# Loading x already transposed by DMA, in place of transposing it on TensorE

The chip is one Trainium2; the program runs on one of its cores. The metric is the device time of one execution in microseconds (us), the median over executions. The kernel was already tuned.

## The reference

With S = 2048 rows, D = 640 and F = 1536, all bf16 (the zero is a scalar zero):

```
h   = einsum("bsd,df->bsf", x, w1) + b1
r   = where(h > 0, h, 0)
out = einsum("bsf,fd->bsd", r * r, w2) + b2
```

In both kernels the first-layer matmuls on TensorE (the PE), 128*128 by 128x256 or 128x512 in the traces, read x with D on the partitions, that is, transposed; x lies in DRAM with rows of D.

## The kernel before

The PE's program is a list of events: dummy matmuls ("D") that keep it busy while the first loads come, transposes of one 128-row tile of x ("T"), first-layer groups ("S1", five matmuls into one PSUM bank) and second-layer tiles ("S2", 24 matmuls). The first groups work on two tiles (256 columns), so that work can begin after the first 256 rows; all later ones work on four tiles (512 columns).

```python
    events += [("D",)] * N_DUMMY_0            # 6
    events += [("T", 0), ("T", 1)]
    events += [("D",)] * N_DUMMY_1            # 1
    events += [S1(t01, 0), ("B1T",), S1(t01, 1)]
    events += [S1(t01, 2), ("T", 2), ("T", 3), S1(t01, 3)]
    events += [S1(t23, 0), S1(t23, 1), S1(t23, 2), S1(t23, 3)]
    # ... four-tile groups 4 to 11, with ("T", 4) to ("T", 7) between them
    # ... later tiles: 12 groups each, with T and S2 events between them
```

All the large loads are issued on SyncE, in this order; each `ld_x` of two tiles and each `ld_w1` is 320 KB, `b2` is 160 KB, the others are 640 KB:

```python
            ld_x(0); ld_w1(0); ld_w1(1); ld_x(1)
            ld_w1(2); ld_w1(3); ld_w1(4); ld_w1(5)
            ld_x(2); ld_w2(0); ld_w2(1); ld_w2(2); b2; ld_x(3); ld_x(4)   # condensed
```

A tile's transposes go to a PSUM bank, and VectorE (DVE) copies them to `xT_sb`, which the first layer reads:

```python
                            ins = pe.transpose(out=pv[:, dt, :],
                                in_=x_sb[:, st, dt * P:(dt + 1) * P], identity=ident[:])
# ...
                        dve.tensor_copy(out=xT_sb[:, pc["lo"]:pc["hi"], st * P:(st + 1) * P],
                            in_=psT_view(pc["bank"])[:, pc["lo"]:pc["hi"], :])
```

## Time and profile before

| | before |
|---|---|
| median time, four executions | 119.98 us (119.90 to 120.22) |
| span of the profiled execution | 118.2 us |
| PE busy | 112.3 us (95%) |
| first real matmul | 5.71 us |
| two-tile groups over | 11.81 us |
| first second-layer tile begins | 25.71 us |
| last five second-layer tiles begin | 99.41 us |

The last four rows are places in the timeline and in the chain of waits. They cut the span into a start (to 11.81), a stretch while loads still come (to 25.71), a steady part (to 99.41) and an end. Such cuts let one see where two kernels differ. The lines of the start stand in the prediction; these are the ones of the cuts, from the chain in order of time (start, duration, engine, line, count of instructions):

```profile
9.46 2.34 PE ps L311 x20
...
25.71 3.26 PE ps L331 x24
...
99.41 16.31 PE ps L331 x120
```

In all these views PE stands for matmuls on TensorE, PEld for its weight loads, DVE for VectorE, ACT for ScalarE, SPq for SyncE issuing a load, and L311 for line 311 of the kernel (the first layer; L331 is the second). One more line is needed later, from the page's part 2:

```profile
DMA packets 10281, 9.46 MB, mean 80 GB/s; under 512 B 545, under 2 KB 10273, under 8 KB 10273
```

### The profile page before, as it was taken

The page shows a single profiled execution, that of the slowest core. Times are in us where ns is not written, and L with a number is a line of the kernel's source. Part 1 is how long each engine was busy: PE and PEld are TensorE (multiplying, and loading weights), DVE is VectorE, ACT ScalarE, POOL GpSimd, SP SyncE. Part 2 cuts the span into 40 slices and gives each one's busy share as a digit, 9 for nine tenths or more (in the row PEclk, how much of TensorE's full clock was granted, in tenths as well). Part 3 has the DMA queues.
Part 4 walks back from the last instruction along what each step waited for, and adds up shares of the span by engine and source line. Part 5 has one row for each costly group of instructions (what it writes and reads, how often), then busy time and mean ns, then how long its engine had stood idle before and what let it go on. Part 6 is the DMA issues. An engine that isn't in the chain of part 4 may idle for free.

```text
span 118.2 us, 1743 instructions
## 1 busy us (share of the span) xinstructions
PE 112.3 (95%) x722; PEld 68.1 (58%) x732; DVE 41.7 (35%) x100; ACT 36.2 (31%) x57; POOL 1.4 (1%) x7
## 2 busy tenths in 40 slices
PE   7698998999999999999999999999999999999991
PEld 2377444456575656657565665647465655777770
DVE  0244354432425434231434534142423334211241
ACT  5156644460423315051422406042332406000000
POOL 4000000000000000000000000000000000000000
DMA  3999999400101001010101001010100101011111
GB/s 74 307 324 309 362 364 367 169 4 0 55 6 55 0 0 58 0 58 6 55 0 47 9 0 61 0 55 0 55 0 19 42 0 55 0 55 55 55 61 55
DMA packets 10281, 9.46 MB, mean 80 GB/s; under 512 B 545, under 2 KB 10273, under 8 KB 10273
## 3 DMA queue, kind: packets, MB, share of 16 engines
q1 hardware_dynamic: 10240, 9.34, 24.8%
q8 instruction: 6, 0.10, 0.4%
q14 instruction: 3, 0.02, 0.0%
q0 software_dynamic: 32, 0.00, 0.0%
HBM read 6.72 MB, written 2.62 MB: 79 GB/s over the span
## 4 chain that ended last, share of the span: by engine, by line
PE 90%; DMA 3%; DVE 3%; ACT 2%; issue 1%
PE ps L331 44%; PE ps L311 42%; PE ps L294 3%; DMA x_sb<-in_x_dram 3%; DVE xT_sb L399 2%; ACT r_sb L380 2%; DVE h2T_sb L407 1%; DVE o_sb L423 0%; PE ps L284 0%
## 5 line engine op out<-in xcount | busy, mean ns | idle before, releaser
L311 PE MATMUL ps<-xT_sb,w_sb 128*128 128x512 bf16 (+1 forms) x250 | 54.3, 362 | 1.5 <-DVE xT_sb L399 0.9
L331 PE MATMUL ps<-w_sb,h2T_sb 128*128 128x320 bf16 x384 | 54.1, 299 | 0.0
L380 ACT ACTIVATE r_sb<-ps,b1T_sb 128x512 bf16<-128x512 f32 (+1 forms) x52 | 34.0, 655 | 59.4 <-PE ps L311 59.1
L331 PEld LDWEIGHTS ps<-w_sb,h2T_sb 128*128 128x128 bf16 x384 | 37.5, 98 | 16.0
L311 PEld LDWEIGHTS ps<-xT_sb,w_sb 128*128 128x128 bf16 x260 | 24.7, 98 | 23.5 <-DVE xT_sb L399 1.5
L407 DVE TENSOR_TENSOR h2T_sb<-r_sb 128x512 bf16<-128x512 bf16 (+1 forms) x52 | 21.1, 405 | 35.6 <-ACT r_sb L380 35.3
L423 DVE TENSOR_TENSOR o_sb<-ps,b_bc 128x320 bf16<-128x320 f32 x32 | 14.3, 487 | 34.2 <-PE ps L331 34.2
L399 DVE COPY xT_sb<-ps 128x640 bf16<-128x640 bf16 (+1 forms) x16 | 7.5, 476 | 4.7 <-PE ps L294 4.7
L294 PEld LDWEIGHTS ps<-ident,x_sb 128*128 128x128 bf16 x80 | 5.5, 101 | 5.7 <-DVE xT_sb L399 1.9
L294 PE MATMUL ps<-ident,x_sb 128*128 128x128 bf16 x80 | 7.0, 225 | 1.2 <-DMA x_sb<-in_x_dram 0.6
L280 PE MATMUL ps<-const-bfloat16-1.0 128*128 128x512 bf16 x7 | 3.1, 588 | 0.8 <-PEq L444 0.8
L280 PEld LDWEIGHTS ps<-const-bfloat16-1.0 128*128 128x128 bf16 x7 | 0.8, 128 | 1.9 <-issue 1.9
L353 ACT ACT_TABLE_LOAD x1 | 1.3, 1283 | 0.7 <-PEq L444 0.7
L363 ACT ACTIVATE xT_sb<-ps 128x128 bf16<-128x128 bf16 x2 | 0.6, 278 | 2.6 <-PE ps L294 2.6
L261 POOL DMA_DIRECT2D b_sb<-in_b_dram x1 | 0.6, 647 | 0.8 <-POOLq L444 0.8
L375 ACT ACTIVATE b1T_sb<-ps 128x12 f32<-128x12 bf16 x1 | 0.2, 182 | 1.2 <-PE ps L284 1.2
L264 POOL TENSOR_SCALAR_AFFINE_SELECT ident<-ident 128x128 bf16<-128x128 bf16 x1 | 0.3, 289 | 0.2 <-POOL ident L262 0.2
L262 POOL MEMSET ident<- 128x128 bf16 x1 | 0.2, 233 | 0.0
L284 PEld LDWEIGHTS ps<-ident,b_sb 12*128 12x128 bf16 x1 | 0.1, 90 | 0.2 <-issue 0.2
L353 ACT ACTIVATE scr_act<-const-float32-0.0 128x1 f32<-128x1 f32 x1 | 0.2, 203 | 0.0
L284 PE MATMUL ps<-ident,b_sb 12*128 12x12 bf16 x1 | 0.2, 176 | 0.0
L444 POOL MEMSET const-bfloat16-1.0<- 128x1 bf16 x1 | 0.1, 108 | 0.0
(3 smaller groups left out, 0.3 us busy)
## 6 DMA issues: line engine op xcount, KB each, us to landing
out_dram<-o_sb SPq DMA_DIRECT2D x15, 160.0 KB, 1.8
w_sb<-in_w_dram SPq DMA_DIRECT2D x6, 320.0 KB, 6.1
x_sb<-in_x_dram SPq DMA_DIRECT2D x3, 640.0 KB, 10.5
w_sb<-in_w_dram SPq DMA_DIRECT2D x3, 640.0 KB, 8.1
x_sb<-in_x_dram SPq DMA_DIRECT2D x2, 320.0 KB, 4.3
b_bc<-in_b_dram SPq DMA_DIRECT2D x1, 160.0 KB, 8.6
out_dram<-o_sb SPq DMA_DIRECT2D x2, 80.0 KB, 1.6
b_sb<-in_b_dram POOLq DMA_DIRECT2D x1, 3.0 KB, 3.7
```

Of the source, the lines that this page charges most:

```text
L261: pool.dma_start(b1_sb[:], b1v).then_inc(sem_b1, 16)
L280: pe.matmul(ps[:, DBANK, :], lhsT=c_lhs, rhs=c_rhs, start=True, stop=True)
L284: pe.transpose(out=psB, in_=b1_sb[:], identity=ident[0:NFT, 0:NFT]).then_inc(sem_peb1, 1)
L294: ins = pe.transpose(out=pv[:, dt, :], in_=x_sb[:, st, dt * P:(dt + 1) * P], identity=ident[:],)
L311: ins = pe.matmul(ps[:, bank, 0:wdt], lhsT=w1_sb[:, dt, ft * P:(ft + 1) * P], rhs=xT_sb[:, dt, s0:s0 + wdt], start=(dt == 0), stop=(dt == ...
L331: return pe.matmul(ps[:, b0 + h, 0:HALF], lhsT=h2T_sb[:, ft, st * P:(st + 1) * P], rhs=w2_sb[:, ft, h * HALF:(h + 1) * HALF], start=(ft == 0),
L353: act.activation(out=scr_act[:, 0:1], in_=c_f32, func=AF.Relu)
L363: act.activation(out=xT_sb[:, pc["lo"]:pc["hi"], st * P:(st + 1) * P], in_=psT_view(pc["bank"])[:, pc["lo"]:pc["hi"], :], func=AF.Copy,).t ...
L380: act.activation(out=r_sb[:, k % NR, 0:wdt], in_=ps[:, k % NS1B, 0:wdt], func=AF.Relu, bias=b1T_sb[:, ft:ft + 1], scale=1.0,).then_inc(sem ...
L399: dve.tensor_copy(out=xT_sb[:, pc["lo"]:pc["hi"], st * P:(st + 1) * P], in_=psT_view(pc["bank"])[:, pc["lo"]:pc["hi"], :],).then_inc(sem_x ...
L407: dve.tensor_tensor(out=h2T_sb[:, ft, s0:s0 + wdt], in0=r_sb[:, k % NR, 0:wdt], in1=r_sb[:, k % NR, 0:wdt], op=ALU.mult,).then_inc(sem_D1, 1)
L423: ins = dve.tensor_tensor(out=o_sb[:, st, h * HALF:(h + 1) * HALF], in0=ps[:, b0 + h, 0:HALF], in1=b2_bc[:, h * HALF:(h + 1) * HALF], op=A ...
```

## The change

The intent is to take the 80 transposes off the PE and the 18 copies off DVE and ScalarE: SyncE issues transposing loads straight into `xT_sb`. The diff, cut to its core:

```diff
-    NS1B = 3
+    NS1B = 4
-    N_DUMMY_0 = 6
-    N_DUMMY_1 = 1
+    N_DUMMY_0 = 9
     events += [("D",)] * N_DUMMY_0
-    events += [("T", 0), ("T", 1)]
-    events += [("D",)] * N_DUMMY_1
     (all other "T" events, their PE transposes and their copies removed too)
         def need_xT_tiles(W, tiles):
             for st in tiles:
-                for pc in tile_pieces[st]:
-                    need_piece_evacuated(W, pc)
+                W.need(sem_x[x_dma_of_tile(st)], 16)
             def ld_x(i):
                 t0, n = x_dmas[i]
-                src = x2[t0 * P:(t0 + n) * P, :].rearrange("(st p) d -> p st d", p=P)
-                sp.dma_start(x_sb[:, t0:t0 + n, :], src).then_inc(sem_x[i], 16)
+                sp.dma_start_transpose(
+                    out=xT_sb[:, :, t0 * P:(t0 + n) * P], in_=x2[t0 * P:(t0 + n) * P, :]
+                ).then_inc(sem_x[i], 16)
```

The order of the loads is unchanged. The bank that held transposes becomes a fourth bank for the first layer.

More of the change, by code (lines that the diff above doesn't have):

```diff
@@ L34, in bass_standalone__dense_activation_squared_relu__prompt_kernel @@
     NR = 4
-    NS1B = 3
-    TBANK = 3
+    NS1B = 4
     S2BANK0 = 4
@@ L39, in bass_standalone__dense_activation_squared_relu__prompt_kernel @@
     B1BANK = 2
-    N_DUMMY_0 = 6
-    N_DUMMY_1 = 1
-    SPLIT_AT = 4
+    N_DUMMY_0 = 9
     x_dmas = [(0, 2), (2, 2), (4, 4), (8, 4), (12, 4)]
@@ L63, in bass_standalone__dense_activation_squared_relu__prompt_kernel @@
     events += [("D",)] * N_DUMMY_0
-    events += [("T", 0), ("T", 1)]
-    events += [("D",)] * N_DUMMY_1
     t01, t23, t03 = [0, 1], [2, 3], [0, 1, 2, 3]
     events += [S1(t01, 0), ("B1T",), S1(t01, 1)]
-    events += [S1(t01, 2), ("T", 2), ("T", 3), S1(t01, 3)]
+    events += [S1(t01, 2), S1(t01, 3)]
     events += [S1(t23, 0), S1(t23, 1), S1(t23, 2), S1(t23, 3)]
-    events += [S1(t03, 4), S1(t03, 5)]
-    events += [S1(t03, 6), ("T", 4), S1(t03, 7), ("T", 5)]
-    events += [S1(t03, 8), ("T", 6), S1(t03, 9), ("T", 7)]
-    events += [S1(t03, 10), S1(t03, 11)]
+    events += [S1(t03, ft) for ft in range(4, NFT)]
     for c in range(1, 4):
@@ L77, in bass_standalone__dense_activation_squared_relu__prompt_kernel @@
             events.append(S1(tiles, g))
-            if c + 1 < 4 and g in (4, 6, 8, 10):
-                events.append(("T", 4 * (c + 1) + (g - 4) // 2))
             if g in (2, 5, 8, 11):
@@ L84, in bass_standalone__dense_activation_squared_relu__prompt_kernel @@
     LAST_S2 = events[-1][1]
-    t_order = [ev[1] for ev in events if ev[0] == "T"]
     s1_groups = [ev[1:] for ev in events if ev[0] == "S1"]
@@ L90, in bass_standalone__dense_activation_squared_relu__prompt_kernel @@
     s2_index = {st: i for i, st in enumerate(s2_order)}
-    assert sorted(t_order) == list(range(NST)) and sorted(s2_order) == list(range(NST))
+    assert sorted(s2_order) == list(range(NST))
     assert len(s1_groups) == len(set(s1_groups))
@@ L99, in bass_standalone__dense_activation_squared_relu__prompt_kernel @@
     tile_last_group = {st: max(cells[(st, ft)] for ft in range(NFT)) for st in range(NST)}
-    def t_pieces(st):
-        if st == 0:
-            return [(0, SPLIT_AT, TBANK, "dve"), (SPLIT_AT, NDT, TBANK + 1, "act")]
-        if st == 1:
-            return [(0, SPLIT_AT, TBANK + 2, "dve"), (SPLIT_AT, NDT, TBANK + 3, "act")]
-        if st == 2:
-            return [(0, NDT, TBANK, "dve")]
-        if st == 3:
-            return [(0, NDT, TBANK + 1, "dve")]
-        return [(0, NDT, TBANK, "dve")]
-    pieces = []
-    for st in t_order:
-        for (lo, hi, bank, eng) in t_pieces(st):
-            pieces.append(dict(st=st, lo=lo, hi=hi, bank=bank, eng=eng))
-    cnt = {"dve": 0, "act": 0}
-    last_in_bank = {}
-    for pi, pc in enumerate(pieces):
-        pc["pe_idx"] = pi
-        pc["prev"] = last_in_bank.get(pc["bank"])
-        last_in_bank[pc["bank"]] = pc
-        cnt[pc["eng"]] += 1
-        pc["evac_cnt"] = cnt[pc["eng"]]
-    tile_pieces = {st: [pc for pc in pieces if pc["st"] == st] for st in range(NST)}
-    EARLY_T_BANK_PIECES = [pc for pc in pieces if pc["bank"] >= S2BANK0]
     s2_pe_after = {}
@@ L159, in sem @@
             return es.enter_context(nc.semaphore(name))
-        x_sb = sb("x_sb", [P, NST, D], BF16)
         xT_sb = sb("xT_sb", [P, NDT, S], BF16)
@@ L186, in bass_standalone__dense_activation_squared_relu__prompt_kernel @@
         sem_b1T = sem("sem_b1T")
-        sem_T = sem("sem_T")
-        sem_xT = sem("sem_xT")
-        sem_xTa = sem("sem_xTa")
         sem_S1 = sem("sem_S1")
@@ L195, in bass_standalone__dense_activation_squared_relu__prompt_kernel @@
         sem_out = sem("sem_out")
-        def psT_view(bank):
-            return ps[:, bank, :].bitcast(BF16)[:, 0:NDT * P].rearrange("p (a b) -> p a b", a=NDT)
         psB = ps[:, B1BANK, :].bitcast(BF16)[:, 0:NFT]
-        evac_sem = {"dve": sem_xT, "act": sem_xTa}
-        def need_piece_evacuated(W, pc):
-            W.need(evac_sem[pc["eng"]], pc["evac_cnt"])
         def need_xT_tiles(W, tiles):
             for st in tiles:
-                for pc in tile_pieces[st]:
-                    need_piece_evacuated(W, pc)
+                W.need(sem_x[x_dma_of_tile(st)], 16)
         @block.sync
@@ L284, in _ @@
                     pe.transpose(out=psB, in_=b1_sb[:], identity=ident[0:NFT, 0:NFT]).then_inc(sem_peb1, 1)
-                elif kind == "T":
-                    st = ev[1]
-                    W.need(sem_ident, 1)
-                    W.need(sem_x[x_dma_of_tile(st)], 16)
-                    for pc in tile_pieces[st]:
-                        if pc["prev"] is not None:
-                            need_piece_evacuated(W, pc["prev"])
-                        pv = psT_view(pc["bank"])
-                        for dt in range(pc["lo"], pc["hi"]):
-                            ins = pe.transpose(
-                                out=pv[:, dt, :],
-                                in_=x_sb[:, st, dt * P:(dt + 1) * P],
-                                identity=ident[:],
-                            )
-                        ins.then_inc(sem_T, 1)
                 elif kind == "S1":
@@ L324, in _ @@
                         W.need(sem_D2, d2_after[s2_order[i - 2]])
-                    for pc in EARLY_T_BANK_PIECES:
-                        need_piece_evacuated(W, pc)
                     b0 = S2BANK0 + 2 * (i % 2)
@@ L356, in _ @@
                 kind = ev[0]
-                if kind == "T":
-                    st = ev[1]
-                    for pc in tile_pieces[st]:
-                        if pc["eng"] != "act":
-                            continue
-                        W.need(sem_T, pc["pe_idx"] + 1)
-                        act.activation(
-                            out=xT_sb[:, pc["lo"]:pc["hi"], st * P:(st + 1) * P],
-                            in_=psT_view(pc["bank"])[:, pc["lo"]:pc["hi"], :],
-                            func=AF.Copy,
-                        ).then_inc(sem_xTa, 1)
-                elif kind == "S1":
+                if kind == "S1":
                     s0, wdt, ft = ev[1:]
@@ L392, in _ @@
                 kind = ev[0]
-                if kind == "T":
-                    st = ev[1]
-                    for pc in tile_pieces[st]:
-                        if pc["eng"] != "dve":
-                            continue
-                        W.need(sem_T, pc["pe_idx"] + 1)
-                        dve.tensor_copy(
-                            out=xT_sb[:, pc["lo"]:pc["hi"], st * P:(st + 1) * P],
-                            in_=psT_view(pc["bank"])[:, pc["lo"]:pc["hi"], :],
-                        ).then_inc(sem_xT, 1)
-                elif kind == "S1":
+                if kind == "S1":
                     s0, wdt, ft = ev[1:]
```

## The prediction

> **What bounds the kernel now.** I read the page first (busy shares and the chain of waits), then the chain in order of time, then the timeline of the first microseconds, then the busy time of the PE in stretches.
>
> ```profile
> PE 112.3 (95%) x722; PEld 68.1 (58%) x732; DVE 41.7 (35%) x100; ACT 36.2 (31%) x57; POOL 1.4 (1%) x7
> ...
> DMA  3999999400101001010101001010100101011111
> ...
> PE 90%; DMA 3%; DVE 3%; ACT 2%; issue 1%
> PE ps L331 44%; PE ps L311 42%; PE ps L294 3%; DMA x_sb<-in_x_dram 3%; DVE xT_sb L399 2%; ACT r_sb L380 2%; DVE h2T_sb L407 1%; DVE o_sb L423 0%; PE ps L284 0%
> ...
> L294 PE MATMUL ps<-ident,x_sb 128*128 128x128 bf16 x80 | 7.0, 225 | 1.2 <-DMA x_sb<-in_x_dram 0.6
> ```
>
> The PE is the bound: it is on the chain for 90% of the span, and nothing else has more than 3%. The DMA engines are full in slices 2 to 7 (to about 21 us) and nearly idle afterwards. L294 is the 80 transposes that the change takes away. Its 7.0 us of busy time are not its price, since neighbouring matmuls overlap there; 3% of the span, 3.6 us, is nearer to it. The chain in order of time gives the unit prices:
>
> ```profile
> 31.12 0.28 PE ps L294 x5
> ...
> 92.92 3.26 PE ps L331 x24
> 96.17 3.24 PE ps L311 x15
> ```
>
> One tile's five transposes cost 0.28 us of PE time in the steady part, a first-layer group over four tiles (five matmuls) 3.24/3 = 1.08 us, and a second-layer tile (24 matmuls) 3.26 us. The start is different. The timeline has:
>
> ```profile
> 0.75 0.43 SPq L217 DMA_DIRECT2D x_sb<-in_x_dram  x1
> ...
> 1.24 1.02 SPq L221 DMA_DIRECT2D w_sb<-in_w_dram  x2
> ...
> 2.30 0.53 SPq L217 DMA_DIRECT2D x_sb<-in_x_dram  x1
> ...
> 2.87 4.43 SPq L221 DMA_DIRECT2D w_sb<-in_w_dram  x4
> ...
> 4.12 0.98 PE L294 MATMUL ps<-ident,x_sb 128*128 128x128 bf16 x10 [0.61 <-DMA x_sb<-in_x_dram]
> ...
> 5.71 0.70 PE L311 MATMUL ps<-xT_sb,w_sb 128*128 128x256 bf16 x5 [0.40 <-DVE xT_sb L399]
> ...
> 9.46 0.71 PE L311 MATMUL ps<-xT_sb,w_sb 128*128 128x256 bf16 x5 [0.54 <-DVE xT_sb L399]
> ```
>
> The first x load is issued at 0.75 and lands at 3.98; ten transposes and the copies out of PSUM follow, and the first real matmul runs at 5.71. The groups over tiles 2 and 3 begin at 9.46 and end at 11.81. The view of issues with their landings, narrowed to single issues, gives 3.9 us for the first w1 block (lands 1.24 + 3.9 = 5.1), 4.8 for the second (1.7 + 4.8 = 6.5), 5.3 for the second x load (2.30 + 5.3 = 7.6) and 5.9 for the third w1 block (8.8). So behind one another, 320 KB land every 1.1 to 1.4 us, as in a queue.
>
> [...] The trace of before has 0.28/5 = 0.056 us of path for one PE transpose in sequence[...]. [...] Before's plain loads moved 316 GB/s in the stretch 5.71 to 11.86. [...]
>
> **The change part by part.**
>
> Removed, steady part (tiles 4 to 15). Between 11.86 and 25.71 the PE does 11 first-layer groups (eight over tiles 0 to 3, three of the next four tiles) and four tiles' transposes: 13.85 - 11 x 1.08 = 1.97 us for the transposes, their switching and their waits for bank 3 to be emptied. Between 25.71 and 99.41 it does 33 groups, 11 second-layer tiles and eight tiles' transposes: 73.70 - 33 x 1.08 - 11 x 3.26 = 2.2 us, which agrees with 8 x 0.28. All of it lies on the path: **4.2 us** saved, 3.5% of the time. The 16 copies on DVE (7.5 us busy) and two on ACT vanish beside the PE, which costs and saves nothing more. A fourth bank for the first layer loosens a wait that the trace does not show; worth nothing.
>
> Removed at the start: ten transposes and their copies between 3.98 and 5.71 (1.7 us), then the second ten (about 0.8 us of path) and a 0.54 us wait for their copies.
>
> Added at the start: x must land transposed, and everything behind it in the queue waits too. The first-layer groups over two tiles need the first x load and the first w1 block; those over tiles 2 and 3 the second x load. I call the transposing rate R. The plain load's 320 KB took 1.1 us behind others. [...] at 150 GB/s 2.2 us (+1.1), at 100 GB/s 3.3 us (+2.2). With d the excess, the first w1 block lands at 5.1 + d, the second x load at 7.6 + 2d. The four groups over tiles 0 and 1 take some 2.6 us, the four over tiles 2 and 3 then 2.35.
> [...]
> - R = 150: first matmul 6.2, second half from 9.8 (the load lands last) to 12.1: 0.3 us lost; 3.9 gained, 116.1 us.
> - R = 100: first matmul 7.3, second half from 12.0 to 14.3: 2.5 us lost, and the last third of w2 comes some 1.4 us late (x of tiles 4 to 7 takes 6.6 us instead of 2.2 ahead of it): about 119.7 us.
>
> Moved: the dummy matmuls are nine in place of seven. At 0.427 us each from 0.79 they end near 4.7, before any of these first matmuls, so they delay nothing and keep the PE busy up to a gap of 0.6 to 2.6 us. All the later x loads have slack: tiles 8 to 15 land before 25 us in the kernel before and are now needed after 48 us.
>
> **The rivals.**
>
> (a) [...] The steady 4.2 us and the start's 1.4 us both come: 113.9 to 114.8 us. [...] Against it: the pieces are 256 B, not the 1280 B rows of before[...].
>
> (b) The transposing load is the new wait. Below about 100 GB/s the wait for x at the start, and again for the next four tiles near 22 us behind a queue in order, eats the 4.2 us. At 60 GB/s a 320 KB load takes 5.5 us (d = 4.4): first matmul at 9.5, after a gap of nearly 5 us[...]; second x load at 16.4; start lost by 7 us, and x and w2 still late afterwards: 124 to 130 us. For it: all loads stand in one queue, and the first slices already run the DMA engines at 90% and more.
>
> (c) SyncE's issue becomes the bound. [...] one issue takes microseconds, the w1 block behind it is issued late, and the start loses 2 to 5 us even though the DMA engines have room: 118 to 121 us.
>
> (d) Nothing is gained, since the transposes were hidden anyway. Against it: they are on the chain, and the PE has under 1% of idle time between 25.71 and 99.41. I leave it little.
>
> **Range and chances.** The removed 4.2 us is near certain; the whole doubt is the start, that is R. I give [...] rather over a quarter to 150 to 220 (115 to 116), a sixth to 110 to 150 (116 to 118.5), and some three tenths to slower loads or slow issues (119 and up, with a long tail). The middle of this is 116.0 us; eight in ten lie between 114.2 and 124.0. Faster by over 2% is below 117.6: 0.65. Within 2% (117.6 to 122.4): 0.13. Slower: 0.22.
>
> **What would show it.** Right: no L294 and no copies into xT; the chain between second-layer tiles holds only 3.24 and 3.26 us pieces; the PE's first real matmul at 5.3 to 6.5 us, released by the DMA of x or w1; a wait on the DMA of x before the groups over tiles 2 and 3 of at most 1.5 us[...]. Wrong: landing of the first x load well over 5 us after its issue, a DMA wait of the PE of several us at the start or near 22 us, issues of several us on SyncE, first matmuls at half clock. If the chain between 26 and 99 us is not about 2.2 us shorter, the removal step is wrong.

## The result, and the profile after

| | before | after |
|---|---|---|
| median time | 120.18 us (16 executions, 119.72 to 121.80) | 116.75 us (11 executions, 115.37 to 118.05) |
| ratio of fast runs | | 0.967 (0.964 to 0.971) |

The ratio is the mean time of one kernel's fast runs over that of the other's of the same rounds, so not quite the ratio of the medians quoted. The kernel is 3.3% faster and it scatters more: its executions lie near 115.4 to 115.8, 116.6 to 117.3 and 118.1 us. The profiled one (118.1 us, span 116.3) belongs to the slow ones. The kernel before has slow executions too, but fewer here: one of sixteen took 121.8 us. First its page: engines, packets and chain by engine and by line (L247 is the first layer, L265 the second):

```profile
PE 110.8 (95%) x645; PEld 65.5 (56%) x654; DVE 35.4 (30%) x84; ACT 35.7 (31%) x55; POOL 1.4 (1%) x7
...
DMA packets 18551, 9.44 MB, mean 81 GB/s; under 512 B 10864, under 2 KB 18544, under 8 KB 18544
...
PE 92%; DMA 4%; SPq 1%; issue 1%; DVE 0%
PE ps L247 47%; PE ps L265 45%; DMA w_sb<-in_w_dram 4%; SPq L166 1%; DVE o_sb L336 0%; PE ps L235 0%
```

The transposes and copies are gone. The chain has two new links at its start: SyncE's issue of the transposing load (L166) and the landing of a **w1** block, not of x. The packets under 512 B grew by 10,319. That fits 2048 rows times five blocks of 128 columns, 10,240 pieces of 256 B: what was a row of 1280 B is now five pieces.

The timeline of the start, of the same kernel (start, duration, engine, line, what):

```profile
0.75 1.34 SPq L166 DMA_TRANSPOSE xT_sb<-in_x_dram  x1
...
0.79 4.00 PE L231 MATMUL ps<-const-bfloat16-1.0 128*128 128x512 bf16 x9 [0.79 <-PEq L357]
...
2.16 1.13 SPq L172 DMA_DIRECT2D w_sb<-in_w_dram  x2
...
6.49 1.23 PE L247 MATMUL ps<-xT_sb,w_sb 128*128 128x256 bf16 x5 [1.70 <-DMA w_sb<-in_w_dram]
...
7.76 6.39 PE L247 MATMUL ps<-xT_sb,w_sb 128*128 128x256 bf16 x35
```

Three things are to be seen. The issue of the first x load takes 1.34 us (0.43 before), so the first w1 block is issued at 2.16 instead of 1.24 and lands at 6.35 (2.16 and 4.2 to landing), while x landed at 4.45 (0.75 and 3.7). The dummies end at 4.79, and the PE stands idle for 1.70 us. And then the matmuls are slow: five of 256 columns take 1.23 us, against 0.70 in the kernel before, and the two-tile groups are over at 14.15 instead of 11.81.

The steady part, in the chain in order of time:

```profile
26.02 3.26 PE ps L265 x24
29.29 3.24 PE ps L247 x15
...
97.50 16.32 PE ps L265 x120
```

From 26.02 to 97.50 are 71.48 us; before they were 73.70 (25.71 to 99.41). Nothing but matmuls of the two layers is left there.

### The profile page after: what moved, and what is told of

Read it like the earlier page. It is cut to its first block, busy times and chain, and to the rows that moved or that the text cites. A ratio compares the mean times of both kernels' runs of the same rounds, so it can differ in the third digit from the quotient of the medians.

```text
span 116.3 us, 1569 instructions
## 1 busy us (share of the span) xinstructions
PE 110.8 (95%) x645; PEld 65.5 (56%) x654; DVE 35.4 (30%) x84; ACT 35.7 (31%) x55; POOL 1.4 (1%) x7
## 4 chain that ended last, share of the span: by engine, by line
PE 92%; DMA 4%; SPq 1%; issue 1%; DVE 0%
PE ps L247 47%; PE ps L265 45%; DMA w_sb<-in_w_dram 4%; SPq L166 1%; DVE o_sb L336 0%; PE ps L235 0%
## 5 line engine op out<-in xcount | busy, mean ns | idle before, releaser
L247 PE MATMUL ps<-xT_sb,w_sb 128*128 128x512 bf16 (+1 forms) x251 | 55.8, 378 | 2.2 <-DMA w_sb<-in_w_dram 1.7
L265 PE MATMUL ps<-w_sb,h2T_sb 128*128 128x320 bf16 x384 | 54.1, 299 | 0.0
L265 PEld LDWEIGHTS ps<-w_sb,h2T_sb 128*128 128x128 bf16 x384 | 37.6, 98 | 16.5
L247 PEld LDWEIGHTS ps<-xT_sb,w_sb 128*128 128x128 bf16 x260 | 26.7, 103 | 28.3 <-issue 2.6
L231 PE MATMUL ps<-const-bfloat16-1.0 128*128 128x512 bf16 x9 | 4.0, 626 | 0.8 <-PEq L357 0.8
```

The costliest lines, as they stand in the source:

```text
L231: pe.matmul(ps[:, DBANK, :], lhsT=c_lhs, rhs=c_rhs, start=True, stop=True)
L247: ins = pe.matmul(ps[:, bank, 0:wdt], lhsT=w1_sb[:, dt, ft * P:(ft + 1) * P], rhs=xT_sb[:, dt, s0:s0 + wdt], start=(dt == 0), stop=(dt == ...
L265: return pe.matmul(ps[:, b0 + h, 0:HALF], lhsT=h2T_sb[:, ft, st * P:(st + 1) * P], rhs=w2_sb[:, ft, h * HALF:(h + 1) * HALF], start=(ft == 0),
```

## The experiments

The state of the PE clock was the suspect for the scatter (the profiler records which share of the full TensorE clock was granted), and the rival was that loads land at varying times. A program on one core is listed as slow when a run is over 1.5% above the fastest of its kernel.

### The changed kernel again

No edit. The first repeat:

> The changed kernel once more, unaltered, because its profiled execution fell in the slow state (116.3 us span) and its runs scatter from 115.4 to 118.1 us while the kernel before stays near 120.2. Theory 1 (the PE starts cold: dummies end at 4.8, the first real matmul comes at 6.5, and after that gap the PE runs its 256-column matmuls at about 213 ns instead of 108 until a moment that differs from execution to execution): a faster execution must show fewer slow 256-column matmuls, and the span must differ by just that; from 26 us on nothing differs. Theory 2 (the loads of x and w1 land at varying times): the first real matmul or a DMA wait moves by the difference, 1 to 2 us. Time 115.4 to 118.1 us again.

Measured: 115.37, 117.00, 117.07 and 117.11 us; ratio 0.969 (0.961 to 0.977). The profiled one was again called slow, but its record of the granted clock shows the cause. The view cuts the time into stretches; columns are the stretch and its length, busy time of PE, PEld, DVE, ACT and POOL, the granted PE clock, DMA share and GB/s:

```profile
6.84:8.00 1.16, 1.16 (x7) 0.64 (x8) 0.00 (x0) 0.00 (x0) 0.00 (x0) 0.59 1.10 195
8.00:9.00 1.00, 1.00 (x7) 0.69 (x7) 0.23 (x1) 0.65 (x2) 0.00 (x0) 0.50 1.12 278
9.00:10.00 1.00, 1.00 (x6) 0.75 (x5) 0.32 (x2) 0.47 (x1) 0.00 (x0) 0.50 1.15 269
10.00:11.00 1.00, 1.00 (x9) 0.78 (x7) 0.23 (x2) 0.47 (x1) 0.00 (x0) 0.77 1.12 303
11.00:12.00 1.00, 1.00 (x11) 0.90 (x10) 0.39 (x2) 0.92 (x2) 0.00 (x0) 1.00 1.20 305
```

The granted clock is one half from about 7.05 to 10.46 us (0.59 and 0.77 are mixtures of 1 and 0.5), one stretch of 3.4 us. Half of that is 1.7 us, which is 1.5% of the span: the mean clock of 0.985 that this run lists. These 1.7 us are also the distance of this execution (117.11) from the fastest (115.37). The start of the same execution:

```profile
0.79 3.50 PE L231 MATMUL ps<-const-bfloat16-1.0 128*128 128x512 bf16 x9 [0.79 <-PEq L357]
6.84 1.05 PE L247 MATMUL ps<-xT_sb,w_sb 128*128 128x256 bf16 x5 [2.55 <-DMA w_sb<-in_w_dram]
```

Nine dummies took 3.50 us here, against 4.00 in the first profile. So the PE had become fast during the dummies, idled for 2.55 us, and lost the clock just as the real work began.

The second repeat asked for a fast run's profile:

> The changed kernel once more, to get a profile of an execution that was not slow. By the theory of the cold PE a fast execution (115.4 us) has the same landings as the slow ones (first w1 block at 6.3 to 6.7, same gap before the first real matmul) but 256-column matmuls of about 108 ns from the first or second group on, so 4.4 to 5.2 us for forty in place of 6.3 to 7.7, and from the first second-layer tile on the same chain.

Measured: 116.83 and 117.16 us, ratio 0.971 (0.963 to 0.979), both with mean clock 0.985. They are called fast only because they are measured against each other; among the executions of the result 117.17 us was called slow. The execution expected at 115.4 did not come, so no execution of that group was ever profiled. The profiled one (span 115.4) took as long as that of the first repeat (115.3), and serves below for the account of the stages. Its stretch view:

```profile
4.80:6.90 2.10, 0.11 (x1) 0.13 (x2) 0.00 (x0) 0.00 (x0) 0.00 (x0) 1.00 1.30 306
6.90:10.40 3.50, 3.50 (x22) 2.47 (x21) 0.88 (x3) 1.61 (x4) 0.00 (x0) 0.66 1.07 257
```

The drop comes a little later here (about 8.0 us, by the same sum), so the first five matmuls ran at full speed (0.70 us) and later ones not. Its gap was 2.03 us and its first matmul came at 6.79 us; the landing of w1 hence moves by 0.3 us between executions (6.35 to 6.7), much less than the scatter. Its chain has these cuts:

```profile
7.61 5.59 PE ps L247 x35
...
25.07 3.26 PE ps L265 x24
...
96.54 16.31 PE ps L265 x120
```

The account of this execution against the kernel before, from the chains: two-tile groups over at 13.20 against 11.81 (1.39 lost), then 11.87 to the first second-layer tile against 13.90 (2.03 saved), then 71.47 against 73.70 (2.23 saved), and an end of 18.86 against 18.79. The sum is 2.80 us, the difference of the spans (118.2 and 115.4).

### Fourteen dummies

```diff
-    N_DUMMY_0 = 9
+    N_DUMMY_0 = 14
```

> Fourteen dummy matmuls in place of nine, nothing else. They end between 6.0 and 6.8 us, so the gap before the first real matmul (6.5) is closed. Theory 1 (cold PE after the gap): the 40 matmuls of 256 columns take 4.4 to 5 us instead of 7.7, the groups over tiles 2 and 3 end near 11 us instead of 14.15, the time falls to 114.3 to 115.3 us and the scatter shrinks to a few tenths. Theory 2 (the loads set the start): no gain, or up to 0.3 us of loss, and the same scatter.

Measured: 115.42 us median of six, from 115.28 to 115.49, 0.1 us above the range of theory 1; ratio 0.960 (0.957 to 0.964). The group of the forty 256-column matmuls (busy time and mean ns after the bar), of the first profile of the changed kernel and then of this one:

```profile
L247 PE MATMUL ps<-xT_sb,w_sb 128*128 128x256 bf16 x40 | 7.6, 375 | 1.7 <-DMA w_sb<-in_w_dram 1.7
```

```profile
L247 PE MATMUL ps<-xT_sb,w_sb 128*128 128x256 bf16 x40 | 4.7, 273 | 0.1
```

The loads were left as they were: in this run the first w1 block landed at 6.4 (2.13 and 4.3). Only the gap was filled with PE work, and the slow matmuls and the scatter of some 2.7 us both vanished. The theory of varying loads falls. The time is that of the fastest executions of the changed kernel (115.37). That these are the ones whose real matmuls ran at full speed is the likely reading; none was profiled. The mean clock alone does not tell: of the twelve executions of the result, the profiled one included, the four from 116.83 to 117.31 us list 0.985; the three fastest list 1.00, but so do three near 116.7 and the two slowest near 118.1.

### A control without any transposing DMA

The kernel before with two dummies in place of six ahead of the first transposes:

```diff
-    N_DUMMY_0 = 6
+    N_DUMMY_0 = 2
```

> The kernel before with two dummy matmuls in place of six ahead of the first transposes: a control for the cold PE without any DMA transpose. The PE then idles from about 1.7 to 4.1 us. If an early idle gap keeps the PE slow for a varying time, this kernel becomes 0.5 to 3 us slower than the kernel before (120.6 to 123 us), with 256-column matmuls of about 213 ns apart well past 6 us, and it scatters as the changed kernel does. If the slow matmuls of the changed kernel have to do with its DMA traffic, this stays at 120 us.

Measured: 121.50 us (121.19 to 121.59), ratio 1.011 (1.009 to 1.014): the same by the 2% rule, but clear of 1. The timeline of this variant:

```profile
0.79 1.01 PE L280 MATMUL ps<-const-bfloat16-1.0 128*128 128x512 bf16 x2 [0.79 <-PEq L444]
3.85 1.23 PE L294 MATMUL ps<-ident,x_sb 128*128 128x128 bf16 x10 [2.06 <-DMA x_sb<-in_x_dram]
...
6.93 2.31 PE L311 MATMUL ps<-xT_sb,w_sb 128*128 128x256 bf16 x10
```

Ten 256-column matmuls take 2.31 us here, about twice the 1.27 us of the kernel before. Too little PE work early on thus makes the PE slow with plain loads too, and transposing loads are not needed for it. The edit lengthens the gap by taking work away, so it does not tell a long gap from little work; nor does the edit to fourteen dummies, which does both the other way round. The expected scatter did not come: all six executions were slow by the same amount. The recorded clock is 1.00 throughout in this run. So there are two forms of the loss: a PE that became fast only late (not seen in the record of the clock, only in the durations; in the first profile of the changed kernel it was slow to about 12 us, and the record read 1.00 while five 256-column matmuls took 1.23 us instead of 0.70), and one that became fast and fell back (seen as 0.985). The unaltered kernel before also has executions near 121.7 us with a recorded clock of 1.00 (one to four of eleven in the three groups of rounds of these experiments). They took about as long as this control; none was profiled, so their cause is not shown.

### Transposing by DMA in the steady part alone

The kernel before, with tiles 0 to 3 untouched and tiles 4 to 15 loaded by transposing DMA:

```diff
             def ld_x(i):
                 t0, n = x_dmas[i]
+                if t0 >= 4:
+                    sp.dma_start_transpose(out=xT_sb[:, :, t0 * P:(t0 + n) * P],
+                        in_=x2[t0 * P:(t0 + n) * P, :]).then_inc(sem_x[i], 16)
+                    return
     (their "T" events removed; their groups wait for sem_x)
```

> The kernel before with only tiles 4 to 15 loaded transposed by DMA; tiles 0 to 3 keep plain loads, PE transposes and copies, so the start is that of before. It prices the steady part alone: by the prediction 4.2 us less than the kernel before, so 115.7 to 116.1 us, with the scatter of the kernel before, and a chain from 11.86 to 97.3 us of matmuls alone. If the transposes were in fact hidden behind something else in the steady part, less is gained; if the transposing loads of later tiles come too late, a DMA wait appears near 20 to 25 us.

Measured: 115.93 us median, 0.964 (0.959 to 0.968); four executions from 115.56 to 115.93 and two slow ones near 117.6, which were not profiled. Beside the kernel before in the same rounds (120.10), that is 4.2 us less, as expected. The chain of this variant, where L314 and L334 are the two layers:

```profile
9.26 14.21 PE ps L314 x75
23.47 3.26 PE ps L334 x24
...
94.94 16.31 PE ps L334 x120
```

After 9.26 us no DMA wait and no copy is left. From there to the last five second-layer tiles are 85.68 us, against 89.95 in the kernel before (9.46 to 99.41), which is 4.3 us less. So 4.2 to 4.3 us is the gain of the steady part, and in the changed kernel the start gave some of it back.

### Plain loads of the same bytes

The changed kernel with plain loads in the place of the transposing ones; the output is wrong on purpose, since the rows aren't transposed.

```diff
-                sp.dma_start_transpose(
-                    out=xT_sb[:, :, t0 * P:(t0 + n) * P], in_=x2[t0 * P:(t0 + n) * P, :]
-                ).then_inc(sem_x[i], 16)
+                src = x2[t0 * P:(t0 + n) * P, :].rearrange("(p a) d -> p (a d)", p=P)
+                src = src.rearrange("p (dt c) -> p dt c", dt=NDT)
+                sp.dma_start(xT_sb[:, :, t0 * P:(t0 + n) * P], src).then_inc(sem_x[i], 16)
```

> The changed kernel with plain loads of the same bytes in the same order in place of the transposing ones (the output is wrong on purpose: the rows are not transposed). It shows what transposing by DMA costs by itself, with the nine dummies kept. The first load then lands at 4.0 and the first w1 block at 5.1 as in the kernel before, so the gap after the dummies (4.8) is 0.3 us. If the cost of the start is in the transposing loads (slower landing, longer issue on SyncE), the first real matmul comes at 5.1 to 5.3, the PE is warm by about 6, and the time is 113.6 to 114.4 us. If the order of loads and the missing transposes alone made the start slow, it stays at 116 to 117 us. SyncE's issue of an x load should fall from 1.34 to about 0.43 us.

Measured: 115.67 us (115.08 to 116.62), 0.965 (0.958 to 0.972). The issue took 0.63 us and the first real matmul came at 5.75 us, both later than expected, after a gap of 1.18 us. The executions fall into two pairs, 115.1 and 116.2 to 116.6. The result lies between the two expectations. The profiled execution (115.2) ran its first matmuls at full speed and lost 0.51 us to a wait for the second w1 block; the slower pair was not profiled, so what of the result is due to the loads and what to the clock stays open. The first real matmul of the changed kernel came at 6.49 to 6.84 us in its three profiles, so in this order of loads the transposing load makes it 0.7 to 1.1 us late (one profile of the plain loads).

### The first w1 block ahead of x

```diff
-    N_DUMMY_0 = 9
+    N_DUMMY_0 = 11
-            ld_x(0)
-            ld_w1(0)
+            ld_w1(0)
+            ld_x(0)
             ld_w1(1)
```

> The changed kernel with the first w1 block issued ahead of the first x load, and eleven dummy matmuls (they end near 5.3 us). In the changed kernel the transposing load held SyncE for 1.34 us, so the first w1 block was issued at 2.16 and landed at 6.35, and it was this that the first real matmul waited for; x itself had landed at 4.45. If the long issue is what makes the start late, w1 now lands at about 4.2 and x near 5.0, the first real matmul comes at 5.1 to 5.6 and the time falls to 114.0 to 114.6 us (fourteen dummies alone gave 115.4). If the DMA engines' rate is what limits the start, both orders deliver the two blocks at the same time, near 6.3, and the time stays at 115.3 to 115.6 us.

Measured: 114.73 us (114.38 to 114.98), 0.956 (0.953 to 0.958). The timeline of this variant:

```profile
0.75 0.45 SPq L172 DMA_DIRECT2D w_sb<-in_w_dram  x1
1.26 1.46 SPq L166 DMA_TRANSPOSE xT_sb<-in_x_dram  x1
```

w1 lands at 4.15 (0.75 and 3.4) and x at 5.36 (1.26 and 4.1). Both are there one microsecond earlier than in the changed kernel (6.35), with the same bytes through the same engines. So it was the long issue in front of w1, and not the rate of the DMA engines, that made the first matmul late. The time is 0.1 us above the expected range; the first five matmuls took 0.95 us, not yet at full speed.

The same with nine dummies asks how much of a gap is harmful:

> The kernel with the first w1 block ahead of the first x load, with nine dummies in place of eleven: a gap of about 0.5 us before the first real matmul (from 4.8 to 5.4) in place of none. If any gap there keeps the PE slow in some executions, the time becomes 114.7 to 117 us with a scatter of over 1 us; if only gaps of well over 1 us do, it stays at 114.5 to 115 us with little scatter.

Measured: 114.37 us (114.18 to 115.51), 0.951 (0.946 to 0.956). It is the fastest version, though its interval overlaps that of eleven dummies. (In these rounds an execution of the kernel before at 121.72 us counts as fast, which lowers this ratio and the next a little.) The gap was longer than expected: the dummies became fast on their way and ended at 4.3, so the PE waited 1.29 us for x, and in the profiled execution the matmuls were at full speed nevertheless. A gap of 1.3 us is thus not a certain loss. One execution of six took 115.5 us; whether the gap was its cause is not shown, since it was not profiled and lists a clock of 0.999. The line of the gap:

```profile
5.57 0.72 PE L247 MATMUL ps<-xT_sb,w_sb 128*128 128x256 bf16 x5 [1.29 <-DMA xT_sb<-in_x_dram]
```

The same with plain loads (eleven dummies, output wrong on purpose, edit as above):

> The kernel with the first w1 block ahead of the first x load and eleven dummies, with plain x loads of the same bytes (the output is wrong on purpose). It prices the transposing loads when the PE is kept warm. Plain x should land near 4.9 in place of 5.36, but the dummies end at 5.4 to 5.6 anyway: if nothing else of the transposing loads is on the path, the time is within 0.3 us of the transposing one (114.7). If the transposing loads still slow the later w1 blocks or the stretch up to 28 us, it is 0.5 us or more faster.

Measured: 115.07 us (114.50 to 115.47), 0.955 (0.950 to 0.960), the same ratio as with transposing loads. The chain of this variant has, near its start:

```profile
1.92 5.50 DMA w_sb<-in_w_dram
...
7.47 3.51 PE ps L247 x30
```

Here the PE waits 0.61 us for the second w1 block. In this order no cost of the transposing loads is left that these intervals (half a per cent, some 0.6 us) could show.

### w1 from ScalarE's queue

```diff
+            (ScalarE, ahead of its table load:)
+            for bi in range(3):
+                c0 = bi * W1CB
+                act.dma_start(w1_sb[:, :, c0:c0 + W1CB], w1v[:, :, c0:c0 + W1CB]).then_inc(sem_w1[bi], 16)
     (SyncE: ld_x(0), ld_x(1), ld_w1(3), ...; eleven dummies)
```

> The first three w1 blocks are issued from ScalarE's queue, beside the x loads on SyncE, with eleven dummies; only SyncE issues transposing loads. If SyncE's issue is the limit, w1 lands near 5.0, x near 4.6, the first real matmul at 5.1 to 5.5, and the time is 113.9 to 114.6 us. If the rate of the DMA engines is the limit, the first matmul stays near 6.3 and the time at 115.3 to 115.6 us. ScalarE's issues take some 1.5 to 2.5 us before its table load, which nothing waits for until 7 us.

Measured: 117.37 us (115.80 to 117.94), 0.973 (0.967 to 0.978): a miss for both expectations. Now x is late (chain of waits):

```profile
0.75 6.29 DMA xT_sb<-in_x_dram
```

x lands at 7.04 instead of 4.45. Three w1 blocks, issued by ScalarE from 0.74 to 2.34 us, were under way at the same time (0.98 MB on a queue of their own, with a median of 5.6 us to landing; all loads together moved 296 GB/s in the slice from 2.85 to 5.70 us), and only the first of them was needed. That x competed with them is the likely reading; no run tests it. The gap was 1.45 us in the profiled execution, which kept its clock and took 115.8 us, as did one other. The remaining four show the clock of 0.985 and took 117.3 to 117.9 us.

### Three banks for the first layer

The kernel with fourteen dummies and `NS1B = 3`.

> Fourteen dummies and three PSUM banks for the first layer as in the kernel before, in place of four. The prediction called the fourth bank worth nothing: 115.3 to 115.6 us, the same as with four banks. If the PE would have waited for ScalarE to empty a bank, a wait of the PE on ScalarE shows and the time is 0.3 us or more longer.

Measured: 115.27 us (115.19 to 115.49), 0.961 (0.958 to 0.963), against 0.960 with four banks. The fourth bank is worth nothing that these runs can tell.

## Why the prediction was right, and where it was not

**The removal was right to a tenth.** 1.97 and 2.2 us were worked out for the two stretches; the profile of the second repeat has 2.03 and 2.23, and the hybrid, which has nothing else of the change, gained 4.2 us. Rival (d), that the transposes were hidden anyway, is out.

**The start decided the rest, as predicted, but by other terms.** The time of 116.0 leaves 4.0 us of gain, so a loss of about 0.2 us there, from a mixture of rates at which x might land (assumed by the author; no trace showed a transposing load yet). The profile of the second repeat shows a loss of 1.39, the first one 2.34, and the fastest executions took what fourteen dummies take, which is a gain of about 0.4 us (4.6 less in the span, 4.2 of it steady).

**The rate R** turned out at or above the better end of what was assumed, where anything moved. In the first profile of the changed kernel, between 26.5 and 28.3 us, only transposing packets moved; the second fence is the kernel before between 14 and 20 us, with plain loads alone:

```profile
DMA packets 1997, 0.50 MB, mean 280 GB/s; under 512 B 1997, under 2 KB 1997, under 8 KB 1997
```

```profile
DMA packets 1766, 2.18 MB, mean 363 GB/s; under 512 B 66, under 2 KB 1766, under 8 KB 1766
```

That is 280 against 363 GB/s. Between two transposing loads, from 24 to 26 us, there was a lull (135 GB/s on average); its cause stays open, and nothing waited for these loads. The first x load landed 0.47 us later than a plain one (4.45 against 3.98), which by the prediction's own sum (1.1 + 0.47 us for 320 KB) is a rate near 210 GB/s. Rival (b), a wait of the PE for x, did not occur in the changed kernel: the groups over tiles 2 and 3 followed without a wait, and so did the later tiles.

**The issue was mis-sized.** The prediction's length for it was the author's estimate, which no trace showed, and a longer issue stood there as rival (c). It is 1.34 us for 320 KB, and behind eight other loads 4.95 us for 640 KB, where the plain load of the kernel before took 0.92 us in the same place. The plain 320 KB issues of the kernel before took 0.43 us for the first, and 0.45 and 0.52 us for the two behind it. It did not become the bound of the whole start, but it made w1, and not x, the load that the first matmul waited for: 6.49 us against the 6.2 at 150 GB/s. The landing sum (5.1 + d) left out that issue.

**The step that failed** is "they delay nothing and keep the PE busy up to a gap of 0.6 to 2.6 us". It treated such a gap as harmless. The gap was 1.70 to 2.55 us, and it cost up to 2.7 us: the changed kernel's 118.1 against 115.4 with the gap filled. Two of the prediction's own signs of being wrong came true with it, first matmuls at half speed and issues of several us on SyncE (2.70 and 4.95 us). Gaps of 2.03 and 2.55 us, shortly after the PE's first work, were each followed by 3.4 us at a granted clock of 0.50 in the two profiles of the changed kernel that show it; after the gap of 1.70 us, in the third, the record stayed at 1.00 and the first five matmuls took 1.23 us. Gaps of 1.29 and 1.45 us were followed by full speed (0.72 us for the first five) in the two executions that were profiled. The runs show that executions of one kernel fall into groups, not what puts an execution into one of them.

So the saving of 4.2 us was foreseen, but that the start took only little of it back is in part luck: x landed earlier than the middle of what was assumed (4.45 us, against 5.1 at 150 GB/s), the w1 block and the clock came out worse, and these roughly offset each other. The measured 116.75 is itself the middle of several groups of executions.

## What to carry to other kernels

A transposing DMA took all transposes off a bound PE here, and the gain could be read from the chain beforehand: path time per tile (0.28 us), not busy time (7.0 us for 16 tiles). What is to be checked is the start: issue the short plain load that the first matmul needs (0.45 us of issue here) ahead of the transposing one, whose issue is long (1.46 us behind it), and look up which load the first matmul then waits for. When the first real matmul moves, move the dummies with it; a scatter wider than that of the kernel before can be a sign that the PE's clock is at stake, as it was here (115.37 to 118.05 us with nine dummies, 115.28 to 115.49 with fourteen).
